# Second norm of an adaLN block: three of its four row groups turned by VectorE block transposes and a trip through memory

## The chip, the cores and the metric

The kernel runs on one core of a Trainium2 chip. The metric is the time of one execution on the device, in microseconds. The kernel before takes 1378.21 us (median of three runs, 1377.38 to 1378.27).

## What is computed

One transformer block: adaptive layer norm, multi-head attention with a residual, a second adaptive layer norm, and a gated MLP that mixes along the sequence. Cut to what matters (x is 2048 x 448, the MLP's half width is 896):

```python
sa, ca, ga, sb, cb, gb = split(silu(c) @ w_mod)
h = layernorm(x) * (1 + ca) + sa
x = x + ga * attention(h)                     # 16 heads of 28, then @ wo
h = layernorm(x) * (1 + cb) + sb              # the second norm: h2
z = gelu(h @ w_in)                            # 2048 x 1792
z1, z2 = z[:, :896], layernorm(z[:, 896:])
g = w_sp @ z2 + b_sp                          # mixes the 2048 rows
x = x + gb * ((z1 * g) @ w_out)
```

All of it is float32 at its ends. The matmuls split each operand into a high part and a low remainder and add eleven products of the parts.

## The kernel before

The order of the instructions on each engine is the order in which the program writes them; nothing reorders them. The engines are TensorE (PE), VectorE (DVE), ScalarE (ACT), GpSimd (POOL) and SyncE (SP), whose queue issues most DMAs in order. A wait at the head of an engine's queue holds everything behind it.

The 2048 rows are taken in four groups of 512, numbered 0 to 3 in the code, and each group as four tiles of 128 rows. The stages in order:

1. First norm, q, k and v, then attention over all heads (until about 866 us).
2. The output projection, tile by tile (`wo_mm`, `wo_add`, 16 tiles t). `wo_mm` does 11 matmuls of 128x448; `wo_add` (L1034) adds them to x on VectorE in place and stores the sum to memory as `x2_scr` for the very end.
3. The second norm per group. `h2_stats(g)` (L1043 to L1047, and `rstd_of`, whose power is on POOL, L170) gives mean and 1/sigma for the group's four tiles. `h2_norm(g)` (L1055) subtracts and scales on VectorE, two instructions a tile: one over the 448 columns, one that writes the last 64 columns a second time behind them, to columns 448 to 511.
4. `h2_group(g)` calls `ln_transpose` (L172 to L199): 16 transposes on PE (L179) turn the four 128x512 tiles into four PSUM banks of 128 features x 512 rows, the chunks c = 0 to 3. For each chunk, in the order 0, 2, 1, 3, ScalarE applies the scale and shift of the features (L186), then copies to the high part (L193), and VectorE subtracts for the low part (`sub`, L150). The result is `h2T[g]`, high and low parts of h2 with features along the partitions.
5. z1: for each group seven units `z1_unit(g, f)` (L1144), 11 matmuls of 128x512 (L1147) that read `h2T[g]` in the order of `STEPS`: both parts of chunks 0 and 2 first, chunk 1 in steps 7 to 9, chunk 3 in steps 10 and 11. ScalarE applies gelu (L1151) and SP stores the result to `z1_scr` (L1152). Units are counted 0 to 27 here.
6. z2 from the same `h2T`, its norm, the mixing by `w_sp`, the gating and the last projection. At the end the rows of x come back from `x2_scr` (`x2_load`).

PSUM has seven banks in rotation for these stages (`bank`), and one more that every eighth projection tile uses. A z1 unit takes a bank again seven units later.

Around the change the program writes: projection tiles 0 to 11, the norm of group 1, tile 12, group 0's transposes, tiles 13 and 14, group 1's transposes, tile 15, then the z1 units; group 2's transposes stand after unit 4 and group 3's after unit 9. The statistics and norms of groups 2 and 3 stand between them. The scale of `w_in`'s second half and of `w_out` (`win_prep`, `wout_part`) is spread over the z1 units too.

Of the kernel before, what the change touches and what calls it, by code (L numbers as in the profile page):

```python
# [8 lines left out]
F32 = mybir.dt.float32  # L9
F32R = mybir.dt.float32r  # L10
AF = mybir.ActivationFunctionType
ALU = mybir.AluOpType
# [4 lines left out]
S, D, H, DH, FH = 2048, 448, 16, 28, 896  # L17
# [3 lines left out]
NG = 4  # L21
# [7 lines left out]
STEPS = STEPS_MAIN + STEPS_Z  # L29
# [70 lines left out]
def tile_adaln_mha_gmlp(ctx, tc, x, wqkv, wo, w_in, w_spT, b_sp, w_out, cT, w_mod0, w_mod, out):  # L100
    nc = tc.nc
    ctx.enter_context(tc.manual_schedule())
    pe, dve, act, pool, sp = nc.tensor, nc.vector, nc.scalar, nc.gpsimd, nc.sync
# [3 lines left out]
    scr = ctx.enter_context(tc.tile_pool(name="scr", bufs=1, space=DRAM))  # L107
# [4 lines left out]
    x2_scr = scr.tile([S, D], F32, name="x2_scr")  # L112
    z1_scr = scr.tile([FH, S], F32, name="z1_scr")
    ws_scr = scr.tile([4 * len(W_SUMS), 128, 512], F32, name="ws_scr")
    wo2_scr = scr.tile([2, 7, 128, D], F32, name="wo2_scr")
    wl_scr = scr.tile([2 * len(W_SUMS), 128, 512], F32, name="wl_scr")

# [7 lines left out]
    cols = {}  # L125
# [8 lines left out]
    def hview(heap, off, a, b):  # L134
        return heap[:, off : off + a * b].rearrange("p (a b) -> p a b", b=b)
# [13 lines left out]
    def sub(eng, dst, a, hi):  # L149
        eng.tensor_tensor(out=dst, in0=a, in1=hi.bitcast(F32), op=ALU.subtract)  # L150
# [16 lines left out]
    def rstd_of(var, rs, n):  # L167

        dve.tensor_scalar(out=rs, in0=var, scalar1=EPS, scalar2=None, op0=ALU.add)  # L169
        pool.tensor_tensor(out=rs, in0=rs, in1=mhalf[:, :n], op=ALU.pow)  # L170

    def ln_transpose(xns, full_pool, dsts, scol, bcol, engs, los=(pool,) * 4, mid=None, after=None):  # L172

        tps = []
        for c in range(4):
            tp = bank("tp")
            tps.append(tp)
            for t in range(4):
                pe.transpose(tp[:, t * 128 : (t + 1) * 128], xns[t][:, c * 128 : (c + 1) * 128], ident)  # L179
        if mid:  # L180
            mid()
        for c in (0, 2, 1, 3):
            tp = tps[c]
            f = full_pool.tile([128, 512], F32, name="hfull")
            if engs[c] is act:
                act.activation(f, tp, AF.Identity, scale=scol[:, c : c + 1], bias=bcol[:, c : c + 1])  # L186
            else:
                engs[c].tensor_scalar(
                    out=f, in0=tp, scalar1=scol[:, c : c + 1], scalar2=bcol[:, c : c + 1], op0=ALU.mult, op1=ALU.add
                )  # L190
            hi = dsts[:, c if c < 3 else 6, :]
            if engs[c] is act:
                act.activation(hi, f, AF.Copy)  # L193
# [309 lines left out]
    x3 = xts[3]  # L503
# [298 lines left out]
    def o_split(c, qb, eng=pool):  # L802
        cs = slice(qb * 512, (qb + 1) * 512)
        if c < 3:
            src = OT[:, 3 + c, cs]
            pool.tensor_copy(OT[:, c, cs], src.bitcast(F32))
# [20 lines left out]
    def wo_mm(t, steps):  # L827
        if t not in wo_ps:
            wo_ps[t] = bank("wo_ps") if t % 8 < 7 else ps_o.tile([128, 512], F32, name="wo_ps", tag="o")
        for a, b in steps:  # L830
            pe.matmul(
                wo_ps[t][:, :D],
                OT[:, a, t * 128 : (t + 1) * 128],
                wos[:, b, :],
                start=(a, b) == STEPS[0],
                stop=(a, b) == STEPS[-1],
            )
# [113 lines left out]
    first = sorted(((t, kb) for t in range(NT) for kb in range(4)), key=lambda a: (max(a[0] // 4, a[1]) // 3, a))  # L951
    first = first + [(t, kb) for t in range(NT, LEAD) for kb in range(4)]
# [22 lines left out]
    for u in range(NU + 1):  # L975
        for fn, a in events.pop(u, []):
            fn(*a)
        j = u + LEAD
# [31 lines left out]
    fh = ctx.enter_context(tc.tile_pool(name="fh", bufs=1))  # L1010
# [4 lines left out]
    h2T = [hview(heapB, g * 3584, 7, 512) for g in range(2)]  # L1015
# [4 lines left out]
    t3 = ph3.enter_context(tc.tile_pool(name="t3", bufs=2))  # L1020

    x3 = {}
# [9 lines left out]
    def wo_add(t):  # L1032
        xt = x3[t]
        dve.tensor_tensor(out=xt[:, :D], in0=xt[:, :D], in1=wo_ps.pop(t)[:, :D], op=ALU.add)  # L1034
        sp.dma_start(x2_scr[t * 128 : (t + 1) * 128, :], xt[:, :D])

    def h2_stats(g, tts=range(4)):
        if g not in mv3:
            mv3[g] = t3.tile([128, 4, 2], F32, name="mv3"), t3.tile([128, 4], F32, name="rs3"), []
        mv, rs, sts = mv3[g]  # L1040
        for tt in tts:
            st = t3.tile([128, 6], F32, name="st3", bufs=4)
            dve.bn_stats(out=st, in_=x3[4 * g + tt][:, :D])  # L1043
            sts.append(st)
        if len(sts) == 4:
            for tt in range(4):
                dve.bn_aggr(out=mv[:, tt, :], in_=sts[tt])  # L1047
            rstd_of(mv[:, :, 1], rs, 4)

    def h2_norm(g):  # L1050
        mv, rs, _ = mv3.pop(g)
        for tt in range(4):
            xt = x3[4 * g + tt]
            for o, i in ((xt[:, D:], xt[:, 384:D]), (xt[:, :D], xt[:, :D])):
                dve.tensor_scalar(  # L1055
                    out=o, in0=i, scalar1=mv[:, tt, 0:1], scalar2=rs[:, tt : tt + 1], op0=ALU.subtract, op1=ALU.mult
                )

    raw_in = {}

# [7 lines left out]
    def wo_tile(t):  # L1068
        wo_mm(t, STEPS)
        wo_add(t)  # L1070
# [46 lines left out]
    for t in range(4):  # L1117
        wo_mm(t, STEPS_Z)
        wo_add(t)
    o_split(3, 2, dve)  # L1120
    for t in range(4, 8):
        wo_mm(t, STEPS_Z)
        wo_add(t)
    o_split(3, 3, dve)
    h2_stats(0)
    h2_stats(1)
    h2_norm(0)
    heapF = dpool.tile([128, 4 * 896], F32R, name="heapF", tag="heapF")
# [4 lines left out]
    heaps = []  # L1133

    def h2_group(g, after=None):
        if g >= 2:
            heaps.append(fh.tile([128, 4 * 896], F32R, name="heap", tag=("heapE", "heapC")[g - 2]))
            h2T.append(hview(heaps[-1], 0, 7, 512))
        xns = [x3.pop(4 * g + t) for t in range(4)]
        ln_transpose(xns, t3b, h2T[g], cols["cb"], cols["sb"], (act,) * 4, (dve,) * 4, None, after)  # L1140

    zbuf = []

# [9 lines left out]

    for t in range(8, 12):
        wo_tile(t)
    h2_norm(1)
    wo_mm(12, STEPS)
    wo_add(12)
    h2_group(0, lambda c: wo_tile(13) if c == 2 else None)
    wo_tile(14)  # L1160

    def last_tile(c):
        if c == 2:
            wo_tile(15)
        h2_stats(2, ((0, 2, 1, 3).index(c),))

    h2_group(1, last_tile)
    h2_norm(2)
    h2_stats(3)
    win_load(0, t3)  # L1170
    win_load(1, t3b)
    wo3 = ph3.enter_context(tc.tile_pool(name="wo3", bufs=2))
# [14 lines left out]
    def wout_store(f):  # L1187
        for i, part in enumerate(wouts.pop(f)):
            sp.dma_start(wo2_scr[i, f], part.bitcast(F32))

    for g in range(NG):
# [301 lines left out]
    x2t = {}  # L1493

    def x2_load(t):
        x2t[t] = wp.tile([128, 512], F32, name="x2l", tag="raw_sp", bufs=RAWS)[:, :D]
        sp.dma_start(x2t[t], x2_scr[t * 128 : (t + 1) * 128, :])

    def y_part(t, end=False):
        ts, uT = slice(t % 4 * 128, t % 4 * 128 + 128), uTs[t // 4]  # L1500
# [17 lines left out]
    for g in range(KS):  # L1518
        p, kt = divmod(g, 4)
# [95 lines left out]
```

## Time and profile before

| | |
|---|---|
| median of three runs | 1378.21 us |
| span of the profiled execution, first to last instruction | 1376.2 us |
| what lies around the span (median of the runs less the span) | 2.0 us |
| PE busy | 1370.9 us, 100% of the span |
| VectorE, ScalarE, POOL busy | 1067.5, 805.1, 359.9 us |
| clock granted to TensorE | 1.000 throughout |
| second norm and z1 | about 880 to 977 us |

The profiled execution's own time is known by its span alone; the 2.0 us around it are worked out from the median of the runs. PE's busy time says that its matmuls follow each other with next to no gap; matmuls are pipelined, so their listed durations overlap and the pace is read from the starts. A releaser behind "<-" is the instruction that ended a wait.

### The profile page before, as it was taken

The numbers are of one execution on the slowest core, as the hardware profiler recorded it, in microseconds if no ns is written. First come the engines' busy times: TensorE is split into PE (matmuls) and PEld (weight loads), VectorE is DVE, ScalarE is ACT, GpSimd is POOL, SyncE is SP. The second block draws the span as 40 slices with busy tenths as digits, with TensorE's granted clock in tenths as the row PEclk, the third lists the DMA queues.
The fourth block names the chain that finished last, engine by engine and source line by source line (L and its number), as shares of the span: only waits on it lengthen the run. The fifth ranks groups of instructions, "written<-read, shape, count | busy, mean of one in ns | idle before, by whom it ended". The sixth has DMA issues, their size and how long they took to land.

```text
span 1376.2 us, 20532 instructions
## 1 busy us (share of the span) xinstructions
PE 1370.9 (100%) x7098; PEld 974.6 (71%) x7098; DVE 1067.5 (78%) x1688; ACT 805.1 (59%) x1472; POOL 359.9 (26%) x367
## 2 busy tenths in 40 slices
PE   9999999999999999999999999999999999999998
PEld 8888655555555555555555554888898888888898
DVE  7898888888888888888888880673367777999752
ACT  6623666676667666766677779464324544555420
POOL 2134335243624264645640002200011000000000
PEclk9999999999999999999999999999999999999999
DMA  8465757777667667777773110535604665788552
GB/s 292 138 172 180 226 143 228 201 220 206 230 197 229 188 226 238 231 207 232 231 218 101 37 44 23 174 142 190 216 16 152 223 202 187 248 281 269 181 174 98
DMA packets 137075, 254.28 MB, mean 185 GB/s; under 512 B 21832, under 2 KB 37322, under 8 KB 134426
## 3 DMA queue, kind: packets, MB, share of 16 engines
q1 hardware_dynamic: 134254, 248.79, 57.7%
q10 hardware_dynamic: 2718, 4.19, 0.9%
q8 instruction: 56, 0.92, 0.3%
q14 instruction: 47, 0.39, 0.1%
HBM read 174.53 MB, written 73.59 MB: 180 GB/s over the span
## 4 chain that ended last, share of the span: by engine, by line
PE 97%; DVE 2%; issue 0%; DMA 0%; ACTq 0%; ACT 0%; POOL 0%; DVEq 0%
PE st_ps L741 19%; PE o_ps L756 17%; PE mt L709 17%; PE z_ps L1373 5%; PE acc L1441 5%; PE acc L1442 5%; PE acc L1440 5%; PE pq L404 5%; PE z_ps L1147 5%; PE pv L386 2%; PE y_ps L1508 2%; PE y_ps L1509 2%; PE y_ps L1507 2%; PE acc L1449 1%; PE acc L1450 1%; PE acc L1448 1%
## 5 line engine op out<-in xcount | busy, mean ns | idle before, releaser
L714 DVE TENSOR_REDUCE pm<-mt 128x1 f32<-128x512 f32 x1024 | 630.6, 680 | 86.1 <-PE mt L709 86.1
L745 ACT ACTIVATE P<-st_ps 128x512 f32<-128x512 f32 x1024 | 515.4, 626 | 202.6 <-PE st_ps L741 201.8
L741 PE MATMUL st_ps<-qst,kst 128*128 128x512 f32 x1024 | 406.3, 406 | 0.0
L709 PE MATMUL mt<-kst,qst 128*128 128x512 f32 x1024 | 402.8, 393 | 0.0
L741 PEld LDWEIGHTS st_ps<-qst,kst 128*128 128x128 f32 x1024 | 191.6, 188 | 140.8 <-issue 93.0
L756 PE MATMUL o_ps<-P,V 128*32 128x512 f32 x2048 | 246.3, 599 | 0.0
L709 PEld LDWEIGHTS mt<-kst,qst 128*128 128x128 f32 x1024 | 192.7, 188 | 31.5
L869 POOL TENSOR_TENSOR ws_raw<-ws_raw 128x512 f32<-128x512 f32 x112 | 143.6, 1288 | 177.7 <-DMA ws_raw<-in_w_spT_dram 110.5
L1357 ACT ACTIVATE heapB<-raw_sp 128x512 fp32r<-128x512 f32 x156 | 96.7, 630 | 98.4 <-PE acc L1442 68.3
L756 PEld LDWEIGHTS o_ps<-P,V 128*32 128x32 f32 x2048 | 53.7, 109 | 122.8 <-issue 117.4
L1442 PE MATMUL acc<-heapB,heapA 128*128 128x512 f32 x312 | 121.5, 390 | 0.0
L1440 PE MATMUL acc<-heapB,heapA 128*128 128x512 f32 x312 | 121.5, 390 | 0.0
L150 DVE TENSOR_TENSOR heapB<-raw_sp,heapB 128x512 fp32r<-128x512 f32 x112 | 74.6, 686 | 28.0 <-ACT heapB L1357 27.8
L1441 PE MATMUL acc<-heapB,heapA 128*128 128x512 f32 x222 | 86.6, 390 | 0.0
L1440 PEld LDWEIGHTS acc<-heapB,heapA 128*128 128x128 f32 x312 | 58.6, 188 | 12.2
L1442 PEld LDWEIGHTS acc<-heapB,heapA 128*128 128x128 f32 x312 | 58.6, 188 | 12.0
L404 PE MATMUL pq<-heapD,heapD 128*128 128x512 f32 x196 | 61.9, 390 | 0.0
L150 POOL TENSOR_TENSOR ws_raw<-ws_raw 128x512 fp32r<-128x512 f32 x44 | 56.6, 1287 | 3.5
L785 POOL TENSOR_TENSOR osb<-osb,rb 128x512 f32<-128x512 f32 x15 | 19.2, 1280 | 112.0 <-DMA rb<-r_scr 93.3
L1441 PEld LDWEIGHTS acc<-heapB,heapA 128*128 128x128 f32 x222 | 41.7, 188 | 8.9 <-DVE heapB L150 0.3
L1376 ACT ACTIVATE z<-z_ps 128x448 f32<-128x448 f32 x32 | 17.4, 544 | 47.7 <-PE z_ps L1373 47.7
L170 POOL TENSOR_TENSOR rsz<-rsz,mhalf 128x1 f32<-128x1 f32 x16 | 14.3, 891 | 118.1 <-DVE rsz L169 118.1
(218 smaller groups left out, 1652.8 us busy)
## 6 DMA issues: line engine op xcount, KB each, us to landing
ws_raw<-in_w_spT_dram SPq DMA_DIRECT2D x136, 256.0 KB
ws_scr<-ws_raw SPq DMA_DIRECT2D x112, 256.0 KB
ws_raw<-ws_scr SPq DMA_DIRECT2D x88, 256.0 KB
raw_sp<-ws_scr SPq DMA_DIRECT2D x88, 256.0 KB
raw_sp<-in_w_spT_dram SPq DMA_DIRECT2D x68, 256.0 KB
wl_scr<-ws_raw SPq DMA_DIRECT2D x44, 256.0 KB
kst<-qk_scr SPq DMA_DIRECT2D x45, 224.0 KB
qst<-qk_scr SPq DMA_DIRECT2D x45, 224.0 KB
```

Source lines behind the costliest of these rows:

```text
L150: eng.tensor_tensor(out=dst, in0=a, in1=hi.bitcast(F32), op=ALU.subtract)
L404: pe.matmul(pq, wqk[:, b, m * 128 : (m + 1) * 128], hT[g][:, a, :], start=j == 0, stop=j == NST - 1)
L709: pe.matmul(mt, qst[h % 3][:, t * 128 : (t + 1) * 128], kst[h % 3][:, kb * 512 : (kb + 1) * 512], start=True, stop=True)
L714: dve.tensor_reduce(out=pms[h][:, t, kb : kb + 1], in_=mt, axis=AX.X, op=ALU.max)
L741: pe.matmul(st, kst[h % 3][:, kt * 128 : (kt + 1) * 128], qst[h % 3][:, qb * 512 : (qb + 1) * 512], start=True, stop=True)
L745: act.activation(p, st, AF.Exp, scale=SCALE)
L756: pe.matmul(otile[h][32 * qb : 32 * qb + 32, :], V[:, kt, h, :], ptiles.pop((u, qb)), start=kt == 0, stop=kt == NT - 1)
L869: pool.tensor_tensor(out=a, in0=a, in1=b, op=ALU.add if W_SUMS[v][2] > 0 else ALU.subtract)
L1357: act.activation(hi, raw[0], AF.Copy)
L1440: pe.matmul(o, zh[:, c], hi, start=p < 2 and kt == 0, stop=False, skip_group_check=p > 1)
L1441: pe.matmul(o, zh[:, c], lo, start=False, stop=False, skip_group_check=p > 1)
L1442: pe.matmul(o, zl[:, c], hi, start=False, stop=kt == 3, skip_group_check=p > 1)
```

## The change

Group 0 is still turned on PE. Groups 1 to 3 (the second to the fourth) take another way:

- **Norm.** For all groups ScalarE now normalises, one instruction a tile over 448 columns, with scale rs and bias nb = -mean * rs; VectorE makes nb once a group. For group 0 POOL copies the last 64 columns behind; the other groups don't need the second copy.
- **Turn** (`h2_turn`). VectorE transposes each tile in blocks of 32x32 into one buffer. The input rows of these groups are laid out by the host in another order (partition 32a+i of tile t holds row 128a+32t+i), so that the blocks of one partition quarter hold 128 rows in order. SP stores the four quarters to `hs_scr` (448 features x 512 rows), in pieces of 512 bytes.
- **Load** (`h2_load`). SP loads the group back with features along the partitions, into the places of the low parts: five DMAs.
- **Split** (`h2_group`). ScalarE's scale and copy and VectorE's subtraction are as before, but read SBUF and not PSUM.
- **Places.** Group 0's statistics and norm come before the adds of tiles 4 to 7, its transposes before tile 12, and tiles 12 to 15 between its four chunks. Group 1's statistics are spread over tiles 8 to 11; its norm and turn stand after group 0's chunks. All the rest is spread over the z1 units by the table `H2_AT`.
- **x2.** The rows of `x2_scr` are now in the changed order within a group; `x2_load` reads them back in the reference's order.

```diff
     def h2_norm(g):
         mv, rs, _ = mv3.pop(g)
+        nb = t3.tile([128, 4], F32, name="nb3")
+        dve.scalar_tensor_tensor(out=nb, in0=mv[:, :, 0], scalar=-1.0, in1=rs, op0=ALU.mult, op1=ALU.mult)
         for tt in range(4):
             xt = x3[4 * g + tt]
-            for o, i in ((xt[:, D:], xt[:, 384:D]), (xt[:, :D], xt[:, :D])):
-                dve.tensor_scalar(
-                    out=o, in0=i, scalar1=mv[:, tt, 0:1], scalar2=rs[:, tt : tt + 1], op0=ALU.subtract, op1=ALU.mult
-                )
+            act.activation(xt[:, :D], xt[:, :D], AF.Identity, scale=rs[:, tt : tt + 1], bias=nb[:, tt : tt + 1])
+            if g == 0:
+                pool.tensor_copy(xt[:, D:], xt[:, 384:D])
+
+    def h2_turn(g):
...
+        for tt in range(4):
+            dve.transpose(blocks[:, :, tt, :], x3.pop(4 * g + tt)[:, :D])
+        for a in range(4):
+            sp.dma_start(
+                hs_scr[g - 1].rearrange("(b j) n -> j b n", j=32)[:, :, a * 128 : (a + 1) * 128],
+                blocks[32 * a : 32 * a + 32].rearrange("p b t i -> p b (t i)"),
+            )
+
+    def h2_load(g):
...
+        for c in (0, 2, 1):
+            sp.dma_start(h2T[g][:, 3 + c, :].bitcast(F32), hs_scr[g - 1][c * 128 : (c + 1) * 128, :])
+        for r in (0, 64):
+            sp.dma_start(h2T[g][r : r + 64, 6, :].bitcast(F32), hs_scr[g - 1][384:D, :])
...
+    o_split(3, 3, dve)
+    h2_stats(0)
+    h2_norm(0)
     for t in range(4, 8):
         wo_mm(t, STEPS_Z)
         wo_add(t)
-    o_split(3, 3, dve)
-    h2_stats(0)
-    h2_stats(1)
-    h2_norm(0)
...
+    def h2_group(g):
+        for c in (0, 2, 1, 3):
+            f, hi = t3b.tile([128, 512], F32, name="hfull"), h2T[g][:, c if c < 3 else 6, :]
+            src = h2T[g][:, 3 + c, :].bitcast(F32)
+            act.activation(f, src, AF.Identity, scale=cols["cb"][:, c : c + 1], bias=cols["sb"][:, c : c + 1])
+            act.activation(hi, f, AF.Copy)
...
     for t in range(8, 12):
         wo_tile(t)
+        h2_stats(1, (t - 8,))
+
+    def late_tile(c):
+        wo_tile({0: 12, 2: 13, 1: 14, 3: 15}[c])
+
+    h2_first(late_tile)
     h2_norm(1)
...
+    h2_turn(1)
     win_load(0, t3)
     win_load(1, t3b)
...
+    H2_AT = {0: ((h2_stats, 2), (h2_norm, 2)), 1: ((h2_load, 1),), 2: ((h2_turn, 2),), 3: ((h2_group, 1),)}
...
     for g in range(NG):
         for f in range(7):
             z1_unit(g, f)
...
-            if g == 0 and f == 4:
-                h2_group(2)
-                h2_norm(3)
-            if g == 1 and f == 2:
-                h2_group(3)
+            for fn, a in H2_AT.get(7 * g + f, ()):
+                fn(a)
```

The rest of `H2_AT` gives, by unit: load of group 2 after unit 4, statistics of group 3 after 5, its norm after 6, its turn after 8, split of group 2 after 9, load of group 3 after 10 and its split after 15.

On PE, from the last projection tile into the z1 units (`tp` is the transposes' bank, `x` and `xl` a group's rows, `z_ps` a z1 unit's bank, `heapB` and `heap` the h2T of groups 0 and 1 and of 2 and 3). Before:

```order
L831 MATMUL wo_ps<-heapD_91,heapD_89 128x448 x4
L831 MATMUL wo_ps<-heapD_91,heapD_90 128x448 x2
L831 MATMUL wo_ps<-heapD_91,heapD_89 128x448 x2
L831 MATMUL wo_ps<-heapD_91,heapD_90 128x448 x3
L1147 MATMUL z_ps<-heapB,heapA 128x512 x55
L179 MATMUL tp<-ident,x_10312 128x128 x16
L1147 MATMUL z_ps<-heapB,heapA 128x512 x55
L179 MATMUL tp<-ident,xl_10267 128x128 x16
L1147 MATMUL z_ps<-heapB,heapA 128x512 x44
L1147 MATMUL z_ps<-heap,heapA 128x512 x154
```

And now:

```order
L832 MATMUL wo_ps<-heapD_94,heapD_92 128x448 x4
L832 MATMUL wo_ps<-heapD_94,heapD_93 128x448 x2
L832 MATMUL wo_ps<-heapD_94,heapD_92 128x448 x2
L832 MATMUL wo_ps<-heapD_94,heapD_93 128x448 x3
L1179 MATMUL z_ps<-heapB,heapA 128x512 x154
L1179 MATMUL z_ps<-heap,heapA 128x512 x154
```

The transposes of groups 2 and 3 are gone from between the z1 matmuls; group 1's, which stood ahead of tile 15, are gone too.

On ScalarE, from the last copy of group 0's split on (`hfull` a scaled chunk, `z1t` the gelu's output). Before, where group 1's split follows directly and group 2's reads the transposes' bank:

```order
L193 ACTIVATE heapB<-hfull 128x512
L1151 ACT_TABLE_LOAD
L1151 ACTIVATE z1t<-z_ps 128x512 x5
L186 ACTIVATE hfull<-tp,col_sb,col_cb 128x512
L193 ACTIVATE heap<-hfull 128x512
```

And now (the `x` rows at L1057 are the norms of groups 1 and 2, the `heapB` rows group 1's split):

```order
L194 ACTIVATE heapB<-hfull 128x512
L1057 ACTIVATE x_10282<-x_10282,nb_10617,rs_10468 128x448 x4
L1183 ACT_TABLE_LOAD
L1183 ACTIVATE z1t<-z_ps 128x512
L1057 ACTIVATE x_10315<-x_10315,nb_10670,rs_10655 128x448 x4
L1183 ACTIVATE z1t<-z_ps 128x512 x3
L1167 ACTIVATE hfull<-heapB,col_sb,col_cb 128x512
L1168 ACTIVATE heapB<-hfull 128x512
```

Two norms now stand in ScalarE's queue: one ahead of unit 0's gelu, one between it and unit 1's; group 1's split comes after unit 3's gelu.

On SP's queue, from the last stores of x on (`turn` is the buffer of transposed blocks). Before:

```order
L1035 DMA x_scr<-xl_10267 128x448 x4
L1063 DMA raw_in<-in_w_in_dram 128x896 x2
L1152 DMA z_scr<-z1t 128x512 x11
L1177 DMA raw_out<-in_w_out_dram 128x448
L1063 DMA raw_in<-in_w_in_dram 128x896
```

And now:

```order
L1036 DMA x_scr<-xl_10270 128x448 x4
L1070 DMA hs_scr_72<-turn 32x14x128 x4
L1090 DMA raw_in<-in_w_in_dram 128x896 x2
L1184 DMA z_scr<-z1t 128x512 x2
L1082 DMA heapB<-hs_scr_72 128x512 x3
L1084 DMA heapB<-hs_scr_72 64x512 x2
L1184 DMA z_scr<-z1t 128x512
L1070 DMA hs_scr_73<-turn 32x14x128 x4
```

The store and the load of group 1 stand in the queue with two loads of weights and two z1 stores between them.

More of the change, by code (lines that the diff above doesn't have):

```diff
@@ L114, in tile_adaln_mha_gmlp @@
     ws_scr = scr.tile([4 * len(W_SUMS), 128, 512], F32, name="ws_scr")
+    hs_scr = [scr.tile([D, 512], F32, name=f"hs_scr{i}") for i in range(1, NG)]
     wo2_scr = scr.tile([2, 7, 128, D], F32, name="wo2_scr")
@@ L1131, in tile_adaln_mha_gmlp, with h2_first @@
     t3b = ph3.enter_context(tc.tile_pool(name="t3b", bufs=2))
[L1133 to L1140, printed above, removed]
+    def h2_first(after):
+        xns = [x3.pop(t) for t in range(4)]
+        ln_transpose(xns, t3b, h2T[0], cols["cb"], cols["sb"], (act,) * 4, (dve,) * 4, None, after)
+    def h2_group(g):
[4 more added lines that the diff above has]
+            act.activation(hi, f, AF.Copy)
+            if c < 3:
+                sub(dve, h2T[g][:, 3 + c, :], f, hi)
+            else:
+                sub(dve, hi[64:128], f[64:128], hi[64:128])
     zbuf = []
@@ L1155, in tile_adaln_mha_gmlp @@
         wo_tile(t)
+        h2_stats(1, (t - 8,))
+    def late_tile(c):
+        wo_tile({0: 12, 2: 13, 1: 14, 3: 15}[c])
+    h2_first(late_tile)
     h2_norm(1)
[L1157 to L1169, printed above, removed]
+    h2_turn(1)
     win_load(0, t3)
@@ L1189, in wout_store @@
             sp.dma_start(wo2_scr[i, f], part.bitcast(F32))
+    H2_AT = {0: ((h2_stats, 2), (h2_norm, 2)), 1: ((h2_load, 1),), 2: ((h2_turn, 2),), 3: ((h2_group, 1),)}
+    H2_AT.update({4: ((h2_load, 2),), 5: ((h2_stats, 3),), 6: ((h2_norm, 3),), 8: ((h2_turn, 3),), 9: ((h2_group, 2),)})
+    H2_AT.update({10: ((h2_load, 3),), 15: ((h2_group, 3),)})
     for g in range(NG):
@@ L1496, in x2_load @@
         x2t[t] = wp.tile([128, 512], F32, name="x2l", tag="raw_sp", bufs=RAWS)[:, :D]
-        sp.dma_start(x2t[t], x2_scr[t * 128 : (t + 1) * 128, :])
+        g, a = divmod(t, 4)
+        if g == 0:
+            sp.dma_start(x2t[t], x2_scr[t * 128 : (t + 1) * 128, :])
+        else:
+            sp.dma_start(x2t[t], x2_scr.rearrange("(g t a i) d -> g a t i d", g=4, t=4, a=4)[g, a])
     def y_part(t, end=False):
@@ L1589, in blocks, with rows_of @@
         return (a if k < 3 else a.transpose(1, 0, 2)).reshape(-1)
+    def rows_of(x):
+        first = x[:512].reshape(1, 4, 128, 448).transpose(0, 2, 1, 3)
+        later = x[512:].reshape(3, 4, 4, 32, 448).transpose(0, 1, 3, 2, 4).reshape(3, 128, 4, 448)
+        return _np.concatenate([first, later])
     lay = {
-        "x": _np.asarray(inputs["A_x"])[0].reshape(4, 4, 128, 448).transpose(0, 2, 1, 3),
+        "x": rows_of(_np.asarray(inputs["A_x"])[0]),
         "wqkv": twice(inputs["A_wqkv"]),
```

9 lines of the change are left out of this document (added).

## The prediction

> **What bounds the kernel now.** I read the busy times and the chain of waits first, then PE's waits.
>
> ```profile
> PE 1370.9 (100%) x7098; PEld 974.6 (71%) x7098; DVE 1067.5 (78%) x1688; ACT 805.1 (59%) x1472; POOL 359.9 (26%) x367
> PE 97%; DVE 2%; issue 0%; DMA 0%; ACTq 0%; ACT 0%; POOL 0%; DVEq 0%
> PE wu L293 <- DVE ones L121: 1.0, 1, 1.0
> PE tp L179 <- DVE x L1055: 0.3, 1, 0.3
> ```
>
> TensorE is busy for 1370.9 of 1376.2 us and its waits add up to 1.3 us. So an instruction taken off PE shortens the run by its pitch, and a wait added to PE lengthens it by the whole wait. Work on other engines costs nothing until PE waits for it. PE's timeline through the second norm (x16 rows are one group's transposes):
>
> ```profile
> 868.30 24.48 PE L831 MATMUL wo_ps<-heapD,heapD 128*128 128x448 f32 x120
> 892.63 0.49 PE L179 MATMUL tp<-ident,x 128*128 128x128 f32 x3
> 893.40 1.71 PE L179 MATMUL tp<-ident,x 128*128 128x128 f32 x13 [0.29 <-DVE x L1055]
> 894.99 4.73 PE L831 MATMUL wo_ps<-heapD,heapD 128*128 128x448 f32 x22
> 899.56 2.09 PE L179 MATMUL tp<-ident,x 128*128 128x128 f32 x16
> 901.41 2.48 PE L831 MATMUL wo_ps<-heapD,heapD 128*128 128x448 f32 x11
> 903.73 12.66 PE L1147 MATMUL z_ps<-heapB,heapA 128*128 128x512 f32 x55
> 916.22 1.91 PE L179 MATMUL tp<-ident,x 128*128 128x128 f32 x16
> 917.88 12.74 PE L1147 MATMUL z_ps<-heapB,heapA 128*128 128x512 f32 x55
> 930.46 1.91 PE L179 MATMUL tp<-ident,xl 128*128 128x128 f32 x16
> 932.12 10.23 PE L1147 MATMUL z_ps<-heapB,heapA 128*128 128x512 f32 x44
> ```
>
> Durations overlap, so I take the distance from one start to the next. Groups 0 to 3 in the code's numbering (the change's "2 to 4" are 1 to 3) hold PE for 2.36, 1.85, 1.66 and 1.66 us. Five z1 units take 916.22 - 903.73 = 12.49, so 2.50 a unit and 0.227 a matmul.
>
> **What goes from PE.** Groups 1 to 3 leave: 1.85 + 1.66 + 1.66 = 5.17. Group 0 stays and can lose its wait: 2.36 - 1.66 = 0.70. Gross gain 5.87 us, if group 0 is ready. PE comes to it one projection tile earlier: 11 matmuls at 24.33 / 119 = 0.204, so at 892.63 - 2.25 = 890.38. Rows for its chain:
>
> ```profile
> 882.02 2.21 DVE L1034 TENSOR_TENSOR x<-x,wo_ps 128x448 f32<-128x448 f32 x4
> 884.98 2.21 DVE L1043 BATCH_NORM_STATS2 st<-x 128x6 f32<-128x448 f32 x4
> 887.50 0.17 DVE L169 TENSOR_SCALAR rs<-mv 128x4 f32<-128x4 f32 x1
> 887.75 1.04 POOL L170 TENSOR_TENSOR rs<-rs,mhalf 128x4 f32<-128x4 f32 x1 [15.38 <-DVE rs L169]
> L186 ACT ACTIVATE hfull<-tp,col_sb,col_cb 128x512 f32<-128x512 f32 x16 | 12.2, 765 | 15.6 <-PE tp L179 12.4 <-DVE heapB L150 3.2
> L1183 ACT ACTIVATE wout<-raw_out 128x448 fp32r<-128x448 f32 x7 | 4.0, 578 | 25.1 <-issue 14.9 <-DVE raw_out L1181 10.2
> L806 POOL CAST heapD<-heapD 128x512 fp32r<-128x512 f32 x12 | 7.3, 610 | 0.0
> ```
>
> Four adds (2.21) move behind the statistics, so these start about 2.25 earlier, near 882.73; the power ends at 888.79 - 2.25 = 886.54. The new nb (128x4, like the 0.17 row) ends near 886.75. ScalarE's norm, 128x448 with a scale and a bias per row, is in no row: from 0.578 (the 448-wide copy) to 0.80 (the 512-wide one with both, plus hand-over). I take 0.70, the 512-wide scaled down. Four end at 889.6, 0.8 before PE comes. POOL's four 64-column copies are each well under the 0.61 of 512 columns, and only the last four transposes, 1.25 us later, need them. So they cost nothing; without that cover PE waits by the excess. The four moved adds end near 889.0. Their banks are needed by group 0's transposes, in that order, from 890.38; they too are covered.
>
> z1 then starts at 903.73 - 0.70 - 1.85 = 901.18.
>
> **What is late next: group 1.** Its first z1 matmul is due at 901.18 + 7 x 2.50 = 918.68; chunk c3 is read in step 10 of 11, so its last part is due at 918.68 + 9 x 0.227 = 920.72. Rows for its chain (the last one, a stretch: busy us and instructions of PE, PEld, DVE, ACT and POOL, then clock, DMA share and GB/s):
>
> ```profile
> 905.80 0.61 DVE L1034 TENSOR_TENSOR xl<-xl,wo_ps 128x448 f32<-128x448 f32 x1
> L1055 DVE TENSOR_SCALAR x<-x,mv,rs 128x448 f32<-128x448 f32 x12 | 6.2, 513 | 0.4
> L1043 DVE BATCH_NORM_STATS2 st<-x 128x6 f32<-128x448 f32 x6 | 3.6, 618 | 0.0
> 907.84 1.28 ACT L1151 ACT_TABLE_LOAD   x1
> 868.50 3.36 DVE L1105 RECIPROCAL rb<-sums 128x512 f32<-128x512 f32 x1 [0.59 <-PE sums L1103]
> L150 DVE TENSOR_TENSOR heapF<-raw_in,heapD 128x896 fp32r<-128x896 f32 x2 | 2.2, 1094 | 0.9 <-ACT heapD L157 0.9
> L1151 ACT ACTIVATE z1t<-z_ps x28: 575/589/612, 909.1 to 977.7; 128x512 f32<-128x512 f32 x28
> L1152 SPq DMA_DIRECT2D z_scr<-z1t x28: 319/320/541, 909.8 to 979.3; - x28
> 938.35 0.33 SPq L1177 DMA_DIRECT2D raw_out<-in_w_out_dram  x1
> 940.96 0.63 DVE L1181 TENSOR_TENSOR raw_out<-raw_out,bc_gb 128x448 f32<-128x448 f32 x1 [1.43 <-DMA raw_out<-in_w_out_dram]
> 943.09 0.42 SPq L1177 DMA_DIRECT2D raw_out<-in_w_out_dram  x1
> 946.76 0.62 DVE L1181 TENSOR_TENSOR raw_out<-raw_out,bc_gb 128x448 f32<-128x448 f32 x1 [2.11 <-DMA raw_out<-in_w_out_dram]
> 916.96 0.77 ACT L186 ACTIVATE hfull<-tp,col_sb,col_cb 128x512 f32<-128x512 f32 x1
> 922.43 0.69 DVE L150 TENSOR_TENSOR heap<-hfull,heap 64x512 fp32r<-64x512 f32 x1 [0.64 <-ACT heap L193]
> 942.00:977.00 35.00, 35.00 (x156) 29.01 (x155) 11.34 (x16) 12.61 (x24) 0.00 (x0) 1.00 0.71 238
> ```
>
> The order fixes the chain. The new load of group 1 stands on SP behind the z1 stores of units 0 and 1, and ScalarE's gelu of unit 1 stands behind the norm of group 2. That norm waits for nb, hence for VectorE, where group 2's statistics stand behind group 1's transposes. So group 1 pays for both norms:
>
> - last add (0.61) ends 902.0, nb 902.2, four norms of 0.70 end 905.0;
> - VectorE follows tile by tile. **A block transpose (128x448) is in no row.** Nearest are 0.513 and 0.618 for 448 columns in and out; the slowest VectorE form here, the reciprocal, would be 3.36 x 448 / 512 = 2.94. I take 0.62, by the nearest rows, so the fourth ends at 905.7;
> - group 2's statistics to the end of the power, 888.79 - 884.98 = 3.81: 909.5; nb 909.7; four norms 912.5. ScalarE's table load (1.28) and the gelu of unit 0 fit between its two norms;
> - gelu of unit 1 (0.59) 913.1, its store (0.32 and hand-over) 913.5, and the load goes out;
> - a load of 224 KB reached its reader after 940.96 - 938.35 = 2.61 and 946.76 - 943.09 = 3.67. I take 3.1 for the first chunk: 916.6;
> - the scale, copy and subtraction of four chunks took from 916.96 to 922.43 + 0.69, 6.16. The source is SBUF now; I keep 6.16: 922.8.
>
> PE therefore waits 922.8 - 920.72 = **2.1 us**, inside the first unit of group 1. The gelus held up on ScalarE meanwhile (units 1 to 6) cost nothing: their seven banks are reused seven units, 17.5 us, later.
>
> The trip out lies under the wait for unit 1's gelu. Four stores of 224 KB leave at 905.7, followed by two loads of 448 KB and a z1 store: 2.1 MB, at the 238 GB/s of the busiest stretch nearby 8.8 us, so through by about 914.8, when the load already stands behind them. That fits 916.6 by little. The stores go in 512-byte pieces, of which no row tells the rate; at half of it they take 3.9 us more, and nearly all of that is wait.
>
> Groups 2 and 3 have room. Group 2 is due from 918.68 + 2.1 + 17.5 = 938.3; ScalarE takes it up after the gelu of unit 9 (PE done near 928.3), behind group 3's norm and three gelus, near 931, and ends 6.2 later at 937, while c3 is due at 940.3. Group 3 has two units more. The 32 VectorE norm instructions that go and ScalarE's 16 that come lie beside PE otherwise. The final x2 loads read the same rows in another order, well ahead of their use, and cost nothing.
>
> **Sum.** -5.87 + 2.1 = -3.8 us, so a span of 1372.4. The runs' median of 1378.21 is 2.0 above the profiled span; I keep these 2.0 and predict **1374.4 us**. Measurement tells about 0.2%, 2.76 us, from no change, so the boundaries are 1375.5 and 1381.0.
>
> **Bounds.** Norm at 0.578 or 0.80: eight in the chain, -1.0 or +0.8. Load: -0.5 or +0.6. Transposes: at 0.513, -0.1; at D over 0.70 they set the pace, 902.2 + 0.70 + 4D, which is 4D - 2.8 later than 905.7. Stores: 0 to +3.9. All low, the wait is 0.5; all of these high but the transposes, about 7.
>
> **A rule on the transposes.** The 896-wide VectorE row, twice the columns, took 1.094. At this price for 448 columns, 4 x 1.094 - 2.8 = 1.6 us more wait and a time of 1376.0. The Trainium skill, page "VectorE: DVE Perf Modes", section "The three transpose paths", gives 311 ns for VectorE on 128x128 in bf16, and that only in blocks of 32x32. By 3.5 times its figure a tile is an estimate of 1.09 us, so by that rule the time is the 1376.0 of the sentence above; no run here shows it yet.
>
> **Rivals.**
> - *Group 1 arrives in time.* The wait is under 0.5, all of 5.87 is kept: 1372.3. It needs every price at its lower end or a faster load. For it: nothing else in the trace holds PE.
> - *The trip through memory is late.* The stores' pieces or the loads ahead of them hold the load; the wait is 3.1 to 8.6. With the 3.9 above: 1378.3, no change.
> - *Transposes at half rate*, D near 1.09: 1376.0, no change.
> - *Transposes slow, the run slower.* VectorE passes four-byte blocks at a rate like the reciprocal's. Up to D = 1.9 only 4D - 2.8 counts. Beyond it group 2's transposes, which stand ahead of group 1's subtractions on VectorE, hold these too: they end 0.7 + 4D after norm 2 starts, while the first subtraction is ready after 2.8 + 0.6 + 0.4 + 3.1 + 1.4 = 8.3. The net change is then (4D - 2.8) + (4D - 7.6) - 3.8 = 8D - 14.2. It passes +2.76 from D = 2.1; at 2.94 it is +9.3, 1387.5. For it: no row of such an instruction. Against: the 448-wide rows lie between 0.51 and 0.62.
>
> **Chances.** Forecast (wait 0.5 to 3.1) 0.40, in time 0.24, trip late 0.14, half rate 0.11, slow transposes 0.11 (with any other way to the slower side). Faster 0.64, same 0.25, slower 0.11. The range takes in the full gain below; above it runs to 1379.0, past the half rate and the trip at half speed, and leaves out the slow transposes and the latest trips.
>
> **What would show it.** Right: 48 fewer PE transposes; group 0's 16 in 1.66 us with no wait; one PE wait of some 2 us at the first z1 unit of group 1, on ScalarE or VectorE of that group, and none at groups 2 and 3; transposes near 0.62; the load of group 1 leaving SP right after unit 1's store. Wrong: PE waiting at group 0 or at group 2, SP waiting for the stores of the turned tile rather than for the gelu, transposes over 1 us, or a z1 start other than 2.5 us earlier.

## The result, and the profile after

| | before | after |
|---|---|---|
| median of the runs beside each other, us | 1378.13 | 1390.59 (1389.92 to 1391.34) |
| ratio, 95% interval | | 1.0091 (1.0077 to 1.0106) |
| span of the profiled execution, us | 1376.2 | 1389.5 |

The changed kernel is 12.5 us slower, where 3.8 us less were forecast. The profiled execution of after is the slowest of its four (1391.34), so the spans differ by 13.3. Busy times of after:

```profile
PE 1371.4 (99%) x7050; PEld 970.5 (70%) x7050; DVE 1064.4 (77%) x1672; ACT 815.9 (59%) x1488; POOL 361.3 (26%) x371
```

The 48 transposes are gone and PE's share fell from 100% to 99%: the added time is waits, and slower matmuls behind some of them (last section). All of PE's listed waits in after:

```profile
PE z_ps L1399 <- ACT z1t L1183: 7.5, 1, 7.5
PE z_ps L1179 <- ACT heapB L1168: 2.5, 2, 1.6
PE z_ps L1179 <- ACT heap L1168: 2.3, 2, 1.5
PE wu L294 <- DVE ones L122: 1.0, 1, 1.0
PE z_ps L1179 <- DVE heapB L151: 0.9, 1, 0.9
```

L1179 are z1's matmuls, `heapB` the h2T of groups 0 and 1, `heap` that of groups 2 and 3. The largest wait is at L1399, the first matmul of z2, for a gelu of z1. PE's timeline of after shows where each sits:

```profile
891.00 1.91 PE L180 MATMUL tp<-ident,x 128*128 128x128 f32 x16
892.66 9.16 PE L832 MATMUL wo_ps<-heapD,heapD 128*128 128x448 f32 x44
901.66 17.63 PE L1179 MATMUL z_ps<-heapB,heapA 128*128 128x512 f32 x77
920.88 0.50 PE L1179 MATMUL z_ps<-heapB,heapA 128*128 128x512 f32 x1 [1.59 <-ACT heapB L1168]
922.25 2.60 PE L1179 MATMUL z_ps<-heapB,heapA 128*128 128x512 f32 x8 [0.86 <-ACT heapB L1168]
925.71 15.71 PE L1179 MATMUL z_ps<-heapB,heapA 128*128 128x512 f32 x68 [0.86 <-DVE heapB L151]
941.25 17.61 PE L1179 MATMUL z_ps<-heap,heapA 128*128 128x512 f32 x77
960.33 0.50 PE L1179 MATMUL z_ps<-heap,heapA 128*128 128x512 f32 x1 [1.46 <-ACT heap L1168]
961.70 19.34 PE L1179 MATMUL z_ps<-heap,heapA 128*128 128x512 f32 x76 [0.86 <-ACT heap L1168]
988.51 1.49 PE L1399 MATMUL z_ps<-heapD,heapB 128*128 128x448 f32 x3 [7.48 <-ACT z1t L1183]
```

The first matmul of z2 in before started here:

```profile
974.84 2.43 PE L1147 MATMUL z_ps<-heap,heapA 128*128 128x512 f32 x10
977.10 0.77 PE L1373 MATMUL z_ps<-heapD,heapB 128*128 128x448 f32 x3
```

Cut at these starts, the spans divide so (z1 in before holds groups 2 and 3's transposes, 3.32):

| stretch on PE, us | before | after | forecast change | measured change |
|---|---|---|---|---|
| up to z1's first matmul | 903.73 | 901.66 | -2.55 | -2.07 |
| z1 (after: 988.51 - 7.48 - 901.66) | 73.37 | 79.37 | -3.32 + 2.1 | +6.00 |
| wait ahead of z2 | 0 | 7.48 | 0 | +7.48 |
| from z2's start to the end | 399.1 | 401.0 | 0 | +1.9 |
| span | 1376.2 | 1389.5 | -3.8 | +13.3 |

In z1, group 0 and 1's fourteen units took 941.25 - 901.66 = 39.59, where fourteen units at 2.50 are 34.97: group 1 lost 4.6. Groups 2 and 3 took 988.51 - 7.48 - 941.25 = 39.78, a loss of 4.8, all from group 3 on. The listed waits are only 5.7 of these 9.4. The rest stands around them: the one matmul between two waits took 0.50 where the pitch is 0.227, the eight behind took 2.60 where 8 x 0.227 is 1.8, and at group 3 PE ran at half clock for some 3.5 us (last section).

### The profile page after: what moved, and what is told of

The parts are those of the page before. It is cut to its first block, busy times and chain, and to the rows that moved or that the text cites. A ratio compares the mean times of both kernels' runs of the same rounds, so it can differ in the third digit from the quotient of the medians.

```text
span 1389.5 us, 20466 instructions
## 1 busy us (share of the span) xinstructions
PE 1371.4 (99%) x7050; PEld 970.5 (70%) x7050; DVE 1064.4 (77%) x1672; ACT 815.9 (59%) x1488; POOL 361.3 (26%) x371
```

## The experiments

The theory formed on this trace: the round that scales `w_out` is late. It goes load of `raw_out` on SP, product on VectorE (L1207), copy on ScalarE (L1209), two gelus, their z1 stores on SP, next load behind them. Two rivals: the turned groups' work on ScalarE costs this time wherever the round stands (A), or the trip through memory does (B). All runs at a glance (waits are PE's listed waits; "before" is run beside each group of kernels, with 1377.34, 1378.15 and 1377.26 us):

| kernel | median, us | ratio to before (95%) | waits in z1 | wait at z2 |
|---|---|---|---|---|
| after | 1390.59 | 1.0091 (1.0077 to 1.0106) | 5.7 | 7.5 |
| after, w_out loads 2 units earlier | 1375.07 | 0.9984 (0.9975 to 0.9994) | 2.0 | 0 |
| before, w_out loads 2 units earlier | 1377.21 | 0.9998 (0.9989 to 1.0008) | 0 | 0 |
| after, w_in loads behind unit 2 | 1390.38 | 1.0093 (1.0078 to 1.0108) | 4.9 | 6.6 |
| after, both | 1374.58 | 0.9979 (0.9970 to 0.9988) | 1.3 | 0 |
| after, split of group 3 at unit 14 | 1387.24 | 1.0064 (1.0050 to 1.0078) | 3.0 | 7.8 |
| after, both, and turns respaced | 1385.24 | 1.0050 (1.0037 to 1.0064) | 8.8 | 0 |
| before, groups 2 and 3 not turned | 1374.98 | 0.9979 (0.9970 to 0.9988) | 0 | 0 |
| the same, w_out loads earlier | 1375.16 | 0.9978 (0.9969 to 0.9987) | 0 | 0 |
| after, oldest bank first at z2 | 1379.62 | 1.0014 (1.0005 to 1.0023) | 4.3 | 0 |
| before, two groups not turned, wrong bank | 1377.12 | 0.9999 (0.9990 to 1.0008) | 0 | 2.3 |
| after, both, oldest bank first | 1375.24 | 0.9982 (0.9973 to 0.9991) | 2.0 | 0 |
| after, oldest bank, split at unit 14 | 1377.60 | 0.9999 (0.9990 to 1.0008) | 2.5 | 0.3 |

### The round of w_out two units earlier, in after and in before

```diff
-            for fn, n in ((wout_load, 10), (wout_part, 11), (wout_store, 12)):
+            for fn, n in ((wout_load, 8), (wout_part, 11), (wout_store, 12)):
```

> The changed kernel with the loads of w_out's blocks issued two z1 units earlier. Theory (the w_out round sets the end: load issue, VectorE's product, ScalarE's copy, two gelus, two z1 stores, then the next load issue, some 5.3 to 6 us for two units where TensorE needs 5.0): the 7.5 us wait of TensorE at the start of z2 falls below 1 us, the 2.3 us at group 3 falls too, and the time comes to 1377 to 1380. Rival A (group 3's split, 5.5 us of ScalarE between the gelus, is what makes the gelus late, whatever the loads do): the wait at z2 stays at 5 us or more, time 1387 to 1389. Rival B (the trip through memory alone): no change within 1 us of 1390.6.

Measured 1375.07 us. PE's waits within z1 and z2 in this run:

```profile
PE z_ps L1179 <- ACT heapB L1168: 1.6, 2, 0.9
PE z_ps L1179 <- DVE heapB L151: 0.4, 1, 0.4
```

The wait at z2 and group 3's are gone, with no instruction less on ScalarE and the same trip through memory, so rivals A and B fall for these two waits. One number of SP's order is worth 15.5 us here by the medians, 14.7 by the ratios to before. That is more than was expected (1377 to 1380): the theory had the right place and too small a price.

> The kernel before with the same two units' earlier loads of w_out. Theory: TensorE had no wait on this round before the change, so the time stays within 1 us of 1378.1. Rival (the round held the kernel before as well): faster by more than 1 us.

Measured 1377.21 against 1377.34: no change. What the move cures costs nothing in the kernel before.

### The loads of w_in behind unit 2

```diff
-    win_load(0, t3)
-    win_load(1, t3b)
...
+            if g == 0 and f == 2:
+                win_load(0, t3)
+                win_load(1, t3b)
```

> The changed kernel with the two 448 KB loads of w_in moved from ahead of unit 0 to behind unit 2, so that they are not ahead of group 1's load in the queue. Theory (queue): group 1's first chunk, which arrived 5.7 us after the issue of its load, arrives after about 3.1 us, and TensorE's wait at group 1 falls from 4.6 to about 2 us; the time moves by less, by 0 to -2.5, because the w_out round sets the end. Rival (the 512-byte pieces of the turned tile hold the load): the chunk still takes 5 us or more and the wait stays above 4 us.

The load of group 1 in after left SP behind these two loads of 448 KB (queue of SP, start and issue time):

```profile
909.09 2.27 SPq L1090 DMA_DIRECT2D raw_in<-in_w_in_dram  x2
911.46 2.04 SPq L1184 DMA_DIRECT2D z_scr<-z1t  x2
913.68 1.37 SPq L1082 DMA_DIRECT2D heapB<-hs_scr  x3
```

and ScalarE got its first chunk 919.35 - 913.68 = 5.67 us later:

```profile
919.35 0.81 ACT L1167 ACTIVATE hfull<-heapB,col_sb,col_cb 128x512 f32<-128x512 f32 x1 [5.25 <-DMA heapB<-hs_scr]
```

In the experiment (SP, then ScalarE) the same takes 915.28 - 912.60 = 2.68:

```profile
912.60 1.29 SPq L1082 DMA_DIRECT2D heapB<-hs_scr  x3
```

```profile
915.28 0.82 ACT L1167 ACTIVATE hfull<-heapB,col_sb,col_cb 128x512 f32<-128x512 f32 x1 [2.28 <-DMA heapB<-hs_scr]
```

So the two loads ahead in the queue made the load late, and not the stores in pieces of 512 bytes by themselves: those stores are the same in both. Group 1's listed waits fell from 3.3 us to 1.1. Yet the median, 1390.38, did not move. Most of what PE saved in group 1 it waited later: group 3's waits rose from 2.3 to 3.8 us, and 6.6 stayed at z2, in the profiled execution, which is the fastest of four (1388.83). The end of z1 was pinned elsewhere.

> The changed kernel with both edits: w_out's loads two units earlier and w_in's loads behind unit 2. Theory: both waits shrink, and the time is 1374 to 1377, below the kernel before. Rival A (group 3's split): 1384 or more. Rival (512-byte pieces): like the early w_out loads alone, 1377 to 1380.

1374.58 us, 0.9979 of before: with both moves the change gains 2.8 us. For the change as it stood 3.8 were forecast.

### Group 3's split one unit earlier

```diff
-    H2_AT.update({10: ((h2_load, 3),), 15: ((h2_group, 3),)})
+    H2_AT.update({10: ((h2_load, 3),), 14: ((h2_group, 3),)})
```

> The changed kernel with group 3's split at unit 14 instead of 15, so that its eight instructions on ScalarE (5.5 us) stand ahead of the w_out copy of the same pair of units and run while that copy's load and product are still under way. Theory (the end of z1 is set by the round raw_out load, product, copy, two gelus, store, next load; the split hurts as far as it is inserted into one lap of this round): most of the split leaves the lap, the wait at z2's first matmul falls from 7.5 us by 2.5 to 5 us and does not vanish, because the round still starts two units late; time 1385.5 to 1388. Rival (the split's 5.5 us of ScalarE are lost wherever they stand): wait unchanged, time within 1 us of 1390.6.

The time, 1387.24, is as the theory said, but not the way to it. The round ended 5.7 us earlier (its last four gelus start at 981.17 and not 986.91), and PE's wait at z2 did not shrink: 7.8 us, since PE lost nothing in group 3 and came to z2 earlier too. So the split's place costs 3.4 us of the median, and the wait at z2 needs another cause.

### Both moves, and the turns respaced

```diff
-    H2_AT = {0: ((h2_stats, 2), (h2_norm, 2)), 1: ((h2_load, 1),), 2: ((h2_turn, 2),), 3: ((h2_group, 1),)}
-    H2_AT.update({4: ((h2_load, 2),), 5: ((h2_stats, 3),), 6: ((h2_norm, 3),), 8: ((h2_turn, 3),), 9: ((h2_group, 2),)})
-    H2_AT.update({10: ((h2_load, 3),), 15: ((h2_group, 3),)})
+    H2_AT = {0: ((h2_load, 1),), 2: ((h2_group, 1),), 3: ((h2_stats, 2), (h2_norm, 2)), 5: ((h2_turn, 2),)}
+    H2_AT.update({6: ((h2_load, 2), (h2_stats, 3)), 7: ((h2_norm, 3),), 9: ((h2_turn, 3),), 10: ((h2_group, 2),)})
+    H2_AT.update({11: ((h2_load, 3),), 16: ((h2_group, 3),)})
```

> The changed kernel with the w_out loads two units earlier, the two loads of w_in rows behind unit 4, and the steps of groups 1 to 3 spread again: load of group 1 already behind unit 0 and its split behind unit 2, the norms of groups 2 and 3 each a few units later and ahead of gaps, the split of group 3 behind unit 16. Theory: nothing of ScalarE or of SP's queue is then late for PE in groups 1 to 3 but what is left of group 1's load; z1 starts 2.3 us earlier than in the kernel before, 48 transposes (3.3 us beyond group 0) are gone, and 0 to 1.5 us of waits stay: 1372.5 to 1374.5, below both kernels. Rival (a loss that comes with ScalarE's load as such, whatever its order): no better than the version with both moves, 1374.6 or above.

A miss: 1385.24 us. Group 1's wait shrank to 0.6, but group 2's load and split came late. ScalarE, SP and PE of this run:

```profile
925.55 2.72 ACT L1057 ACTIVATE x<-x,nb,rs 128x448 f32<-128x448 f32 x4 [4.34 <-DVE nb L1054]
```

```profile
938.65 1.29 SPq L1082 DMA_DIRECT2D heap<-hs_scr  x3
```

```profile
942.61 0.80 PE L1179 MATMUL z_ps<-heap,heapA 128*128 128x512 f32 x1 [5.38 <-ACT heap L1168]
```

Group 2's norm stood at ScalarE's head for 4.34 us, since its nb needs VectorE, which came to group 2's statistics only behind group 1's subtractions. Behind the norm stood the gelus, and behind their stores on SP stood the stores of group 2's turned tiles and its load. The load then waited 2.6 us more until those stores had landed, and PE waited 5.4 us. These rows show an order that is worse than that of the version with both moves; they show no loss by ScalarE's load as such.

### The kernel before, with two groups not turned

```diff
-        for c in range(4):
+        for c in range(4 if turn else 0):
...
-        ln_transpose(xns, t3b, h2T[g], cols["cb"], cols["sb"], (act,) * 4, (dve,) * 4, None, after)
+        ln_transpose(xns, t3b, h2T[g], cols["cb"], cols["sb"], (act,) * 4, (dve,) * 4, None, after, g < 2)
```

> The kernel before, with the transposes of groups 2 and 3 left out altogether: ScalarE's split reads a tile of group 2 as it is, so the z1 of these two groups is computed of other data. PE has 32 transposes less (3.3 us by the rows of the kernel before), and no other engine has more to do. The w_out loads stay where they are. Theory (the round of w_out on ScalarE and SP ran at PE's own pace already in the kernel before, and ended exactly with PE): the gain is well below 3.3 us, and a wait of 1.5 to 4 us appears at z2's first matmul: 1375.5 to 1378. Rival (the round binds only because the change loads ScalarE): the full gain, 1374.0.

> As the run before (the kernel before without the transposes of groups 2 and 3, other data in these two groups), and the w_out loads two units earlier. Theory: the limit is out of the way, the whole 3.3 us of transposes are gained and PE has no wait at z2: 1373.5 to 1374.5. Rival (the transposes lay in PE's pace with something else than w_out's round): as the run before.

My theory fell here: 1374.98 and 1375.16, some 3.0 to 3.2 us less than before in both, nearly the whole gain (the second is 0.7 above what it was expected to take), and no wait at z2. ScalarE's last gelus in before, then ScalarE's last gelus and PE's first z2 matmul in the run with w_out where it was:

```profile
976.32 2.04 ACT L1151 ACTIVATE z1t<-z_ps 128x512 f32<-128x512 f32 x4
```

```profile
976.22 2.04 ACT L1151 ACTIVATE z1t<-z_ps 128x512 f32<-128x512 f32 x4
```

```profile
975.76 0.77 PE L1373 MATMUL z_ps<-heapD,heapB 128*128 128x448 f32 x3
```

The gelus are no earlier, and z2 started while the last four of z1 were still to come. So z2 does not need the last gelus, and the late round alone is no reason for a wait. In after, z2 started only behind the third of the last four, which ended near 988.4:

```profile
986.91 2.04 ACT L1183 ACTIVATE z1t<-z_ps 128x512 f32<-128x512 f32 x4
```

What differs is the PSUM bank that z2's first unit takes. z2 begins with an order written by hand, in code that the change does not touch:

```python
    banks[:] = [5, 3, 6, 4, 0, 1, 2]
```

Each group's transposes used four banks of the ring of seven. The change takes 12 uses out, and 12 is 7 + 5, so z1 ends with the ring turned by five. Bank 5 was the oldest, that of unit 21, in before. In after it is that of unit 26. The new theory: lateness of the gelus times this list makes the wait.

### The oldest bank first

```diff
-    banks[:] = [5, 3, 6, 4, 0, 1, 2]
+    banks[:] = [2, 6, 3, 0, 4, 5, 1]
```

> The changed kernel with one line more: the hand-written list of PSUM banks that z2 starts with is put in the order in which z1 left them, the longest unused first. In the changed kernel, 12 bank uses for transposes are gone, and by the old list z2's first unit takes the bank of z1's unit 26, the third from the end; in the kernel before it took that of unit 21. Theory (lateness of the gelus alone costs PE nothing at z2, with seven banks between them; it is the list that turns the lag into a wait): w_out's round is as late as before, the last four gelus still start near 987, but z2's first matmul follows z1's last with 0 to 0.6 us of wait; 7 us of wait and 1 to 2 us of slow clock behind it go: 1381 to 1383. Rival (ScalarE is simply that much behind, and z2 needs it within a unit or two): the wait moves to the next units, 1387 or above.

1379.62 us, 11.0 less than after by the medians and 10.6 by the ratios to before; 1381 to 1383 was expected. PE's timeline and ScalarE's of this run:

```profile
940.59 17.61 PE L1179 MATMUL z_ps<-heap,heapA 128*128 128x512 f32 x77
958.44 0.50 PE L1179 MATMUL z_ps<-heap,heapA 128*128 128x512 f32 x1 [0.24 <-ACT heap L1168]
...
963.27 15.71 PE L1179 MATMUL z_ps<-heap,heapA 128*128 128x512 f32 x68 [0.86 <-DVE heap L151]
978.82 0.77 PE L1399 MATMUL z_ps<-heapD,heapB 128*128 128x448 f32 x3
```

```profile
984.01 0.58 ACT L1209 ACTIVATE wout<-raw_out 128x448 fp32r<-128x448 f32 x1 [3.58 <-issue]
984.50 2.04 ACT L1183 ACTIVATE z1t<-z_ps 128x512 f32<-128x512 f32 x4
```

Against PE the gelus are as late as they were: that of unit 24 starts at 984.50, some 13.2 us after PE finished the unit (978.82 less three units of 2.50), against 13.4 in after (986.91 less 973.5). PE goes into z2 without a wait all the same. Of the gain, 7.5 is the wait, 1.9 what came behind it (last section), and 1.7 a shorter z1 (978.82 - 901.13 = 77.69), which no expectation named and which the list, used only from z2 on, does not explain. So 9.4 us of the gain are read at z2 itself.

> The kernel before without the transposes of groups 2 and 3 (other data in these two groups), which took 1374.98 us, with one line changed: in z2's list of banks the first is now that of z1's unit 26 instead of unit 22. Theory (list of banks): the gelu of unit 26 ended 1.9 us behind the start of z2 in that run, so z2's first matmul now waits about 2 us, and time goes up by 2 to 3 us to 1377 to 1378. Rival (the list plays no part): 1375.0 as before.

The other way round, in the kernel before with two groups not turned (waits, then PE's timeline):

```profile
PE z_ps L1373 <- ACT z1t L1151: 2.3, 1, 2.3
```

```profile
976.18 1.22 PE L1373 MATMUL z_ps<-heapD,heapB 128*128 128x448 f32 x3 [2.33 <-ACT z1t L1151]
...
980.08 0.78 PE L1373 MATMUL z_ps<-heapD,heapB 128*128 128x448 f32 x3
```

Two numbers of the list, exchanged, bring the wait into a kernel that has nothing of the change: 1377.12 instead of 1374.98, 0.9999 of before instead of 0.9979.

### The rest of the bill

Two more kernels. The first has both moves, the list and the split at unit 16; the second has the list and the split at unit 14. Of their edits, the new lines for the list and, in the first, for the split:

```diff
-    H2_AT.update({10: ((h2_load, 3),), 15: ((h2_group, 3),)})
+    H2_AT.update({10: ((h2_load, 3),), 16: ((h2_group, 3),)})
...
-    banks[:] = [5, 3, 6, 4, 0, 1, 2]
+    banks[:] = [2, 6, 3, 0, 4, 5, 1]
```

> The changed kernel with w_out's loads two units earlier, the loads of w_in rows behind unit 2, the banks in the order of their age at z2, and group 3's split behind unit 16 instead of 15. Theory: as the version with both moves (1374.6), which had no wait at z2 and 1.3 us in groups 1 and 3; the bank list adds nothing where the gelus are in time, group 3's 0.4 us goes: 1373.5 to 1374.7. Rival (the gelus' lag still costs something at z2): below 1373.5.

1375.24, half a microsecond above what was expected, and 0.9982 of before (0.9973 to 0.9991): not to be told from the version with both moves, 0.9979. Where the gelus are in time the list plays no part. Group 3's 0.4 us did not go (0.9 and 0.2 are left at `heap`), so this split was no better placed at 16.

> The changed kernel with the banks in the order of their age at z2 and group 3's split at unit 14, w_out's loads and the loads of w_in rows where the change has them. Theory (three causes that add up: the bank list, group 3's split behind the w_out copy, group 1's load behind two others): what is left is group 1's late load, about 4.6 us by the trace of the changed kernel against 1.2 in the version with both moves; time 1390.6 minus 8 to 9.5 for the list minus 3.3 for the split: 1377.5 to 1379.5. Rival (the parts overlap, each fix uncovers the other's wait): 1381 or above.

1377.60, where 1377.5 to 1379.5 was expected: the causes nearly add up. In after alone the list was worth 11.0 us and the split 3.4, which would give 1376.3; beside the list the split was worth 2.0. With the two moves it is 2.4 to 3.0 us less still.

## Why the prediction was wrong

- **Group 0 and z1's start: right.** The 16 transposes took 892.66 - 891.00 = 1.66 with no wait, and z1 started 2.07 us earlier, 2.55 forecast.
- **Prices on ScalarE and VectorE: right in size.** These rows of after are the norm and the block transpose:

```profile
L1057 ACT ACTIVATE x<-x,nb,rs 128x448 f32<-128x448 f32 x8 | 5.4, 751 | 7.4 <-DVE nb L1054 7.4
```

```profile
L1068 DVE STREAM_TRANSPOSE turn<-x x8: 645/646/648, 903.4 to 912.7; 128x448 f32<-128x448 f32 x8
```

0.75 where 0.70 was taken, and 0.646 where 0.62 was. With 0.646, both rivals of the transposes fell. By the Trainium skill, page "VectorE: DVE Perf Modes", section "The three transpose paths", the estimate was 1.09, scaled with the columns. The trace does not agree with that scaling; the Trainium skill's own figure, for bf16 and 128x128, no run here tests.
- **Group 1: right mechanism, wrong size.** The load reaches its reader after 5.67 us, where 3.1 was taken, so the loss was 4.6 and not 2.1. The text had counted the 2.1 MB ahead and called the fit "by little"; it took the price from loads that had no other ahead. The run with the loads of w_in moved measures 2.68. The rival "the trip through memory is late" describes this by its "loads ahead of them"; its other half, the stores' pieces, is not borne out. That its 1378.3 lies near the 1379.62 of the run with the banks in order is in part luck: this run also holds a loss at group 3 that the rival did not have.
- **"Groups 2 and 3 have room": half wrong.** Group 2 had (no wait at 941.25). Group 3's split stands on ScalarE behind the w_out copy, which waits for VectorE's product and that for a load. The sum had that copy in a row, for its price, but did not place it in ScalarE's order. The copy, the first of the split and the next copy in after:

```profile
958.33 0.58 ACT L1209 ACTIVATE wout<-raw_out 128x448 fp32r<-128x448 f32 x1 [3.69 <-issue]
958.82 0.80 ACT L1167 ACTIVATE hfull<-heap,col_sb,col_cb 128x512 f32<-128x512 f32 x1
969.11 0.58 ACT L1209 ACTIVATE wout<-raw_out 128x448 fp32r<-128x448 f32 x1 [3.77 <-DVE raw_out L1207]
```

Waits of 2.3 us and a loss of 4.8 followed, where the sum had nothing. The split also stretched one lap of the round, from copy to copy, to 969.11 - 958.33 = 10.78 us; the same lap in before took 6.13 (copies at 958.24 and 964.37).
- **"Their seven banks are reused seven units, 17.5 us, later": the step that failed.** The prediction wrote it for units 1 to 6, where it holds, and had no term for the lag of the last units. At the border to z2 the order is another list, fitted to a ring that 12 uses of the transposes had turned. Taking these away, z2's first bank was that of unit 26, reused two units later, 5 us after this unit's start on PE. Its gelu started some 9.4 us after PE had finished the unit (987.9 against 978.5), and PE waited 7.48. With the lag as it is, this list cost 11.0 of the 12.5 us; with the lag gone (w_out loads earlier) the same list costs nothing. So it takes both, and either cure is enough. No term of the sum priced the banks at this border and no rival named them, though they are what the transposes on PE hold besides its time.

So the slower side came true by a mechanism that was not among the rivals; the chances held it only as "any other way to the slower side". With the list in order, the change as it stands is 0.14% slower than before (0.05 to 0.23). With the w_out loads earlier, under either list, it is about 0.2% faster, 1374.58 to 1375.24 in three versions: 2 to 3 us, where 3.8 were forecast.

What stays open: why the z1 of after was 1.7 us longer than with the list in order, with the same program up to there (1.2 of it is the wait ahead of group 3's first matmul, 1.46 against 0.24), and how much of the gelus' lag came from the round's place against PE and how much from the split.

## What to carry to other kernels

An instruction that is taken out also gives back what it held: count its buffers, and follow the ring of buffers to the next place where an order was fitted by hand, also far behind the change. An engine's lag is free only as far as the next reuse of what it has to empty, so compare the lag with the reuse distance at each border between stages. And price a load by what stands ahead of it in its own queue, not by the same load elsewhere.

## What the runs showed of the hardware

PE did not come out of its waits at full pace. z2's first matmuls in after, behind the 7.48 us:

```profile
989.80 0.58 PE L1399 MATMUL z_ps<-heapF,heapB 128*128 128x448 f32 x1
990.17 1.32 PE L1399 MATMUL z_ps<-heapD,heapB 128*128 128x448 f32 x3
...
992.78 0.80 PE L1399 MATMUL z_ps<-heapD,heapB 128*128 128x448 f32 x3
993.42 0.37 PE L1399 MATMUL z_ps<-heapF,heapB 128*128 128x448 f32 x1
```

From 988.51 to 992.78 eleven matmuls took 4.27 us, 0.39 each; from 992.78 on three took 0.64, 0.21 each. At that pace the eleven take 2.3, so the wait cost 2.0 us more behind it, which is about the 1.9 of the table. The clock granted to TensorE by windows of after (start and end, length, busy time and instructions of PE, then clock, DMA share and GB/s) says the same, and shows a second such stretch behind group 3's waits:

```profile
958.70:964.00 5.30, 2.97 (x8) 0.82 0.04 14
964.00:988.00 24.00, 17.02 (x71) 0.93 0.61 202
988.00:1060.00 72.00, 71.49 (x343) 0.97 0.22 76
1060.00:1150.00 90.00, 90.00 (x399) 1.00 0.65 218
```

Behind the wait of only 2.33 us in the run with the wrong bank, eleven matmuls took 980.08 - 976.18 = 3.90 us. The Trainium skill, page "TensorE: Matmul & The Clock Gate", part 1, has the array at half its clock after an idle window of about 3.4 us, until it has been busy for as long. The half pace and, roughly, its length agree with these rows; here 2.33 us of waiting were enough.

Still less was enough in z1, and the same waits did not always do it. By stretches of one microsecond, the granted clock of after was 0.56, 0.50, 0.50 and 0.73 from 962 to 966, behind group 3's waits of 1.46 and 0.86 us with one matmul between them. Behind group 1's of 1.59, 0.86 and 0.86 it stayed at 1.00. In the run with the oldest bank first it was the other way round: 0.50 from 922 to 925, behind group 1's 1.12 and 0.87, and 1.00 at group 3. So in these runs the length of a wait alone does not tell whether the clock falls.
